# Eleven short warming products, two more ahead of the fifth block, and block loads that wait for an earlier load

## The chip, the cores and the metric

The kernel runs on one core of one Trainium2 chip. The metric is device time in microseconds (us). The engines are TensorE (PE, with its weight loads as PEld), VectorE (DVE), ScalarE (ACT), GpSimd (POOL) and SyncE (SP), whose queue (SPq) issues nearly all DMAs here.

## The reference

Three stages in a row, on 1536 tokens (2 batches of 768) with 8 heads of 64:

```python
state = gamma * state + k_t outer v_t          # per head, token after token
y_t   = scale * q_t . state                    # retention
x = y as (1536, 512)
h = x @ w_in;  g = h * tanh(softplus(h));  x = g @ w_out          # 512 -> 2048 -> 512
x = (sigmoid(x @ w_gate) * (x @ w_val)) @ w_out2                  # 512 -> 1536 -> 512
```

All weights come as 64-bit floats.

## The kernel before, in words

**Retention** works on 12 blocks of 128 tokens, six for each batch. A block needs two loads of 512 KB: `qk` (queries and keys, features on partitions) and `nv` (keys and values, tokens on partitions). They land in the pool `ld`, which has four buffers of each (`AHEAD = 4`). POOL scales the values by the decay table `ck` (`at_prep`, tile `vp`). PE makes the scores (`sc`), DVE masks them into `a`, PE adds the block's keys times `vp` to the running state (`st`, in PSUM), ACT copies the state out (`s`, in `keep`), and PE makes the output (`ao`) from `a` with `vp` and from `qk` with `s`. DVE multiplies `ao` by the decay `og` into `acc`.

Blocks 0 to 3 (the first four, `T = 4`) are written one after another with products over 128 tokens (`at_scores`, `at_state`, `at_out`). From block 4 (the fifth) a block's scores and state are made in two halves of 64 tokens, of 64x64 products (`scores`, `state`, `outs`), and the products of two blocks alternate (`lanes`, `block`). Between such blocks stand pieces of the first MLP (`dense`, tiles `hx` and `h`, `SHARE[n]` pieces after a block).

**Weights** arrive as pieces of 128 x 512 64-bit words (`raw`, 512 KB, two buffers, `load_piece`). ACT and DVE turn a piece into a 32-bit tile `v`, and ACT and DVE or POOL split that into a high and a low part (`ww`, `wo`).

**Order.** Each engine's instructions keep the order in which the code issues them (`Queue.issue` chains each to the one before). All of the retention stage is in that written order: loads first (`load(0)` to `load(3)`), then after block j of the first four `load(j + 4)`, and in the later loop `load_nv(j + 4)`, `load_qk(j + 3)` and the next weight piece (`feed`). SP issues them in this order, and a DMA waits in SP's queue for its buffer to be free. After the blocks, the rest (both MLPs) is collected as nodes and put in order by a planner (`replay`) from fixed costs.

**Warming products.** Before block 0, PE multiplies a tile of zeros (`z`) by itself five times, 128 x 128 by 128 x 256, into two PSUM buffers that nothing reads. A product of plain 32-bit operands shows as two weight loads and two passes in the trace, so these five are ten rows of each.

The helper `issue` is the one place that calls an engine, so nearly every row of the trace is at its line, L147; groups are told apart by their tiles.

Of the kernel before, what the change touches and what calls it, by code (L numbers as in the profile page):

```python
# [9 lines left out]
F32 = mybir.dt.float32  # L10
# [8 lines left out]
P = 128  # L19
# [4 lines left out]
def kernel(ctx, tc, qk, nv, w1i, w1o, w2g, w2v, w2o, ma_in, og_in, sg_in, ck_in, mh_in, out):  # L24
# [14 lines left out]
    NP = KK  # L39
    D = P // 2  # L40
    FF1 = w1i.shape[0]
    FF2 = w2g.shape[0]
    N = 512
# [3 lines left out]
    RINGS = {"w": 7, "o": 4, "q": 2}  # L47
    H = DM // 2
    STG = 2
    WARM = 5  # L50
    AHEAD = 4
    Q = P // 2
    SHARE = (4, 4, 3, 3, 2, 2, 4, 5, 5)
# [117 lines left out]
    pe = Queue(nc.tensor, lambda n, kw: (kw["rhs"].at.size + 32) / 2400, 0.2)  # L171
    dve = Queue(nc.vector, span(0.1, 0.00102), 0.2)
    act = Queue(nc.scalar, lambda n, kw: 0.14 + 0.0008 * min(n, N), 0.2)
    pool = Queue(nc.gpsimd, slow, 0.2)
    sync = Queue(nc.sync, lambda n, kw: 1.4 if isinstance(kw["out"], Part) else 1.6, 3.5)
# [120 lines left out]
    ps_o = Pool(name="ps_o", bufs=2, space=PSUM)  # L296
# [46 lines left out]
    for f in range(FF2):  # L343
# [3 lines left out]
        a, q, w, o = [[(k, (2, f))] for k in "aqs"] + [[("o", (2, f - 1)), ("o", (2, f))] if f % 2 else []]  # L347
# [103 lines left out]
    def flush_hi():  # L451
        while late_hi:
            late_hi.pop(0)()
# [7 lines left out]
    def pump(n=1):  # L461
        if not early:
            flush()
        for _ in range(n):
            if not steps and not plan():
                return
            ring = steps[0][0]
            if not room(ring) if ring else "dcs" not in lo_eng:
                return
            steps.pop(0)[1]()  # L470
# [59 lines left out]
    hx = {}  # L530
# [215 lines left out]
    def run(*parts):  # L746
        for p in parts:
            for s in p:
                s()
# [22 lines left out]
    with ExitStack() as actx:  # L772
        ac = actx.enter_context(tc.tile_pool(name="ac", bufs=1))
# [8 lines left out]
        ck = ac.tile([P, SPB, 2 * NP, 1], F32, name="ck")  # L782
        sg = ac.tile([P, SPB, NP, 1], F32, name="sg")
        og_t = [ac.tile([P, NP, P], F32, name=f"og{b}") for b in range(SPB)]
        qk_t, nv_t, a_t, vp_t, st_t, s_t, sc_t, o_t = {}, {}, {}, {}, {}, {}, {}, {}

        def load_qk(j):
            if j < NSUB:
                qk_t[j] = ld.tile([P, 2, NP, P], F32, tag="qk", name="qk_t")
                sync.dma_start(out=qk_t[j], in_=qk[j])  # L790

        def load_nv(j):
            if j < NSUB:
                nv_t[j] = ld.tile([P, 2, 2 * NP, D], F32, tag="nv", name="nv_t")
                sync.dma_start(out=nv_t[j], in_=nv[j])

        def load(j):
            load_qk(j)
            load_nv(j)
# [14 lines left out]
        def rows(n):  # L814
            return slice(Q * n, Q * n + Q)

        def quarter(o, w, x, start=True, stop=True):
            pe.matmul(out=o, lhsT=w, rhs=x, start=start, stop=stop, skip_group_check=True)
# [24 lines left out]
        def state(j, s):  # L843

            if j >= NSUB:
                return [lambda: [quarter(st_t[0][rows(c), 0, :], z[rows(0), rows(0)], z[rows(0), rows(0)]) for c in range(2)]]
            v, k = vp_t[j], nv_t[j]
            new = j % SPB == 0 and s == 0
            if new:
                st_t[0] = ps_s.tile([P, NP, D], F32, tag="s", name="st")  # L850
            st = st_t[0]

            def pair(p):
                for e in range(2):
                    quarter(st[rows((e + p) % 2), p, :], k[rows(s), 0, 2 * p + e, :], v[rows(s), 2 * p + e, :],
                            new and p == 0, p == NP - 1)

            return [lambda p=p: pair(p) for p in range(NP)]

        def keep(j, s):  # L860
            s_t[2 * j + s + 1] = at6.tile([P, NP, D], F32, tag="s", name="s")
            act.activation(out=s_t[2 * j + s + 1], in_=st_t[0], func=AF.Copy)
# [95 lines left out]
        act.activation(out=sig, in_=one_t, func=AF.Mish)  # L958
        z = ac.tile([P, NP * D], F32, name="z")
        dve.memset(ap=z, constant=0.0)  # L960
        for n in range(WARM):
            o = ps_o.tile([P, NP * D], F32, tag="o", name="warm")
            pe.matmul(out=o, lhsT=z[:, 0:P], rhs=z)
        def work(n):
            for _ in range(n):
                dense.pop(0)()
# [11 lines left out]
        for j in range(T):  # L978
# [13 lines left out]
            if j == T - 2:  # L992
                pump()
        flush_hi()
        run(state(T, 0))
        keep(T, 0)
        lanes(scores(T + 1, 0), scores(T + 1, 1))
# [9 lines left out]
        decays(T)  # L1007
        decays(T + 1)
        load_nv(T + AHEAD)
        pump()  # L1010
        work(SHARE[0] - 1)
# [5 lines left out]
        for j in range(T + 1, NSUB + 1):  # L1017
            block(j, middles.get(j, lambda: None))
            load_nv(j + AHEAD)
            load_qk(j + AHEAD - 1)  # L1020
            if j < NSUB and j != 2 * SPC:
                feed()
            if j == NSUB:
                flush()
            for n in range(SHARE[j - T]):
                if j == NSUB:
                    lo_eng["g"] = dve if n > 2 else pool
                    run(late_g)
                    late_g.clear()
                work(1)  # L1030
# [24 lines left out]
    for i in range(I0, L1 + 1):  # L1055
        n = len(rest) if i < L1 else 8
# [17 lines left out]
    for f in range(2, FF2):  # L1074
        n = 4 if f < 4 else 6
# [3 lines left out]
        if f == FF2 - 1:  # L1079
            n = 3  # L1080
# [64 lines left out]
```

## Time and profile before

| | us |
|---|---|
| three runs | 581.82, 583.6, 579.15 |
| their median | 581.82 |
| the profiled execution, its own time | 578.88 |
| its span, first to last instruction | 577.0 |
| PE busy in it | 568.1 (98%) |

The profiled execution has 1.9 us beside its span. In the rows, "x" is a count, times are us from the span's start, "idle before <-releaser" is how long the engine waited ahead of the row and what ended that wait, and PEclk or the clock column is the granted clock of TensorE as a share of its upper level.

### The profile page before, as it was taken

To read this page: it belongs to the slowest core of one execution; us is meant where nothing else is said; L and a number is where in the kernel's file an instruction comes from. 1 tells how busy PE (TensorE), PEld (TensorE's weight loads), DVE (VectorE), ACT (ScalarE), POOL (GpSimd) and SP (SyncE) were. 2 spreads that over 40 slices of the span, in tenths; PEclk is the share of its full clock that TensorE was granted. 3 is DMA by queue.
4 is the path that set the end of the run, shared out by engine and by line. 5 is a ranking of instruction groups with operands and counts; after the bars stand their busy time and mean duration, and the time that the engine had idled before them with its cause. 6 is when DMAs were issued, how large, how long until landed. Compare 5 with 4: busy or idle time off the path is not lost.

```text
span 577.0 us, 9810 instructions
## 1 busy us (share of the span) xinstructions
PE 568.1 (98%) x3880; PEld 479.2 (83%) x3880; DVE 458.9 (80%) x680; ACT 294.4 (51%) x544; POOL 219.1 (38%) x198
## 2 busy tenths in 40 slices
PE   8899999999999999999999999999999999999997
PEld 6777888888888888888888878888888888888885
DVE  3877599898998787778988888789888788775574
ACT  1566677585645545355665677545346254231210
POOL 3455588533522300024597554423245043020000
PEclk9999999999999999999999999999999999999999
DMA  9984202422332222112100233221322222000014
GB/s 344 404 294 159 76 0 74 136 86 77 105 110 73 74 73 74 37 39 108 37 1 0 91 128 111 74 87 59 110 74 73 74 73 74 1 0 2 0 38 181
DMA packets 15741, 52.40 MB, mean 91 GB/s; under 512 B 2128, under 2 KB 2256, under 8 KB 15696
## 3 DMA queue, kind: packets, MB, share of 16 engines
q1 hardware_dynamic: 14976, 51.39, 25.5%
q8 instruction: 30, 0.49, 0.3%
q10 hardware_dynamic: 720, 0.40, 0.2%
q14 instruction: 15, 0.12, 0.1%
HBM read 48.63 MB, written 3.15 MB: 90 GB/s over the span
## 4 chain that ended last, share of the span: by engine, by line
PE 95%; DMA 3%; DVE 1%; issue 0%; POOL 0%; SPq 0%; ACT 0%; POOLq 0%; DVEq 0%
PE h L147 37%; PE o L147 37%; PE hx L147 17%; DMA nv_t<-nv 3%; PE ao L147 2%; PE st L147 1%; PE sc L147 1%; DVE h L147 0%; POOL vp L147 0%; SPq L147 0%; DVE acc L147 0%; DVE ww L147 0%; ACT e L147 0%; POOLq L147 0%; DVEq L147 0%
## 5 line engine op out<-in xcount | busy, mean ns | idle before, releaser
L147 PE MATMUL o<-g,wo 128*128 128x512 f32 x492 | 119.1, 391 | 0.0
L147 DVE TENSOR_TENSOR acc<-o,acc 128x512 f32<-128x512 f32 x126 | 86.9, 690 | 39.5 <-PE o L147 37.7
L147 PE MATMUL o<-wo,g 128*128 128x512 f32 x432 | 108.6, 392 | 0.0
L147 PEld LDWEIGHTS o<-g,wo 128*128 128x128 f32 x492 | 90.3, 188 | 17.4
L147 PE MATMUL h<-B,ww 128*128 128x512 f32 x372 | 94.4, 390 | 0.0
L147 PE MATMUL h<-T,ww 128*128 128x512 f32 x366 | 92.9, 390 | 0.1
L147 PEld LDWEIGHTS o<-wo,g 128*128 128x128 f32 x432 | 78.5, 189 | 14.7 <-DVE g L147 0.3
L147 PEld LDWEIGHTS h<-T,ww 128*128 128x128 f32 x366 | 68.4, 188 | 15.1 <-ACT e L147 0.5
L147 PEld LDWEIGHTS h<-B,ww 128*128 128x128 f32 x372 | 68.9, 188 | 13.9
L147 DVE SCALAR_TENSOR_TENSOR raw<-raw 128x512 int32<-128x512 int32 x68 | 61.9, 912 | 2.2 <-ACT raw L147 2.0
L147 ACT ACTIVATE raw<-raw 128x512 int32<-128x512 uint8 x68 | 45.6, 670 | 34.3 <-DMA raw<-w2v 9.1
L147 DVE SCALAR_TENSOR_TENSOR v<-v,raw 128x512 int32<-128x512 int32 x68 | 58.5, 865 | 3.1 <-ACT v L147 0.8
L147 PE MATMUL hx<-xc,ww 128*128 128x256 f32 (+1 forms) x342 | 58.3, 307 | 0.0
L147 POOL TENSOR_TENSOR ww<-s,ww 128x512 fp32r<-128x512 f32 x22 | 30.1, 1371 | 67.8 <-ACT ww L147 67.8
L147 PEld LDWEIGHTS hx<-xc,ww 128*128 128x128 f32 x342 | 50.6, 190 | 5.4 <-DVE ww L147 0.3
L147 POOL TENSOR_TENSOR wo<-v,wo 128x512 fp32r<-128x512 f32 x16 | 21.1, 1330 | 86.2 <-ACT wo L147 49.7
L147 DVE TENSOR_TENSOR h<-h,u 128x512 f32<-128x512 f32 x54 | 37.6, 697 | 15.9 <-PE h L147 14.9
L147 ACT ACTIVATE e<-h 128x512 f32<-128x512 f32 x29 | 17.3, 596 | 59.4 <-PE h L147 48.2
L147 ACT ACTIVATE v<-raw 128x512 f32<-128x512 f32 x68 | 45.1, 666 | 2.1 <-POOL wo L147 1.2
L147 PEld LDWEIGHTS hx<-YT,ww 128*128 128x128 f32 x270 | 38.3, 190 | 3.5
L147 PE MATMUL hx<-YT,ww 128*128 128x256 f32 x270 | 39.4, 282 | 0.0
L147 ACT ACTIVATE g<-h 128x512 fp32r<-128x512 f32 x53 | 31.4, 597 | 14.9 <-DVE h L147 13.9
(97 smaller groups left out, 836.4 us busy)
## 6 DMA issues: line engine op xcount, KB each, us to landing
raw<-w1i SPq DMA_DIRECT2D x16, 512.0 KB, 3.3
raw<-w1o SPq DMA_DIRECT2D x16, 512.0 KB, 3.4
qk_t<-qk SPq DMA_DIRECT2D x12, 512.0 KB, 6.7
nv_t<-nv SPq DMA_DIRECT2D x12, 512.0 KB, 6.8
raw<-w2g SPq DMA_DIRECT2D x12, 512.0 KB, 3.2
raw<-w2v SPq DMA_DIRECT2D x12, 512.0 KB, 3.3
raw<-w2o SPq DMA_DIRECT2D x12, 512.0 KB, 3.3
out<-acc SPq DMA_DIRECT2D x12, 256.0 KB, 2.0
```

The source lines that it names most:

```text
L147: i = call(**kw)
```

## The change

There are three parts:

- The five warming products of 256 columns become eleven of 128 columns, all into one PSUM buffer.
- Two more such products stand on PE between the scores of block 4 and its first state product `state(T, 0)`. They write the PSUM bank `x0`.
- Every load of `qk` or `nv` is noted in `sent`. From the fifteenth on (`qk` of block 7 is the first), SP first issues a copy of one 32-bit word into the new tile `mark`, read from the tile that was noted two entries earlier. The copy can't be issued before the load that fills this tile has landed, and the block's load stands behind the copy in SP's queue. With the current load counted, that is the third one back.

```diff
-    WARM = 5
+    WARM = 11
...
+        mark, sent = ac.tile([P, 32], F32, name="mark"), []
...
+        def paced(t):
+            sent.append(t)
+            if len(sent) > 2 * AHEAD + 6:
+                n = len(sent) % 32
+                sync.dma_start(out=mark[:1, n:n + 1], in_=sent[-3][:1])
...
                 qk_t[j] = ld.tile([P, 2, NP, P], F32, tag="qk", name="qk_t")
+                paced(qk_t[j][:, 0, 0, :1])
                 sync.dma_start(out=qk_t[j], in_=qk[j])
...
                 nv_t[j] = ld.tile([P, 2, 2 * NP, D], F32, tag="nv", name="nv_t")
+                paced(nv_t[j][:, 0, 0, :1])
                 sync.dma_start(out=nv_t[j], in_=nv[j])
...
-        for n in range(WARM):
-            o = ps_o.tile([P, NP * D], F32, tag="o", name="warm")
-            pe.matmul(out=o, lhsT=z[:, 0:P], rhs=z)
+        def warm(pool, tag, n):
+            o = pool.tile([P, N], F32, tag=tag, name="warm")
+            for _ in range(n):
+                pe.matmul(out=o[:, :P], lhsT=z[:, :P], rhs=z[:, :P])
+
+        warm(ps_o, "o", WARM)
...
         flush_hi()
+        warm(hx["pool"], "x0", 2)
         run(state(T, 0))
```

On PE the difference stands in two places. At the program's start (`warm` is the warming product, `sc` and `st` are scores and state of block 0):

```order
-L147 MATMUL warm<-z 128x256 x5
+L1154 UNCONDITIONAL_BRANCH
+L147 MATMUL warm<-z 128x128 x11
 L147 MATMUL sc<-qk_t 128x128 x8
 L147 MATMUL st<-vp,nv_t 64x64 x8
```

Five products became eleven of half the width, and what follows is as before. At the fifth block (`ao` ends block 3, `sc` are the scores of block 4, then its first state product and the scores of block 5):

```order
@@ -17,4 +17,5 @@
 L147 MATMUL ao<-qk_t,s 64x128 x8
 L147 MATMUL sc<-qk_t 64x64 x16
+L147 MATMUL warm<-z 128x128 x2
 L147 MATMUL st<-vp,nv_t 64x64 x8
 L147 MATMUL sc<-qk_t 64x64 x16
```

Two products came in between scores and state, and nothing changed places. On SP, from the loads of block 6 on (`qk_t` and `nv_t` are block loads, `raw` is a weight piece, `mark` the small copy):

```order
 L147 DMA qk_t<-qk 128x1024
 L147 DMA nv_t<-nv 128x1024
+L147 DMA mark<-qk_t 1x1
 L147 DMA qk_t<-qk 128x1024
+L147 DMA mark<-nv_t 1x1
 L147 DMA nv_t<-nv 128x1024
 L147 DMA raw<-w1i 128x512
+L147 DMA mark<-qk_t 1x1
 L147 DMA nv_t<-nv 128x1024
 L147 DMA raw<-w1i 128x512
+L147 DMA mark<-nv_t 1x1
 L147 DMA nv_t<-nv 128x1024
```

Ten copies came in, each ahead of a block load; the last stands ahead of `qk` of block 11. On DVE, ACT and POOL, and on PE elsewhere, the rows are those of before in the same order.

## Rows read from the trace of the kernel before

**Rows 1.** The page: busy time per engine, TensorE's clock and DMA in 40 slices.

```profile
PE 568.1 (98%) x3880; PEld 479.2 (83%) x3880; DVE 458.9 (80%) x680; ACT 294.4 (51%) x544; POOL 219.1 (38%) x198
...
PEclk9999999999999999999999999999999999999999
DMA  9984202422332222112100233221322222000014
```

**Rows 2.** Busy us by stretch: PE, PEld, DVE, ACT, POOL, then clock, DMA share, GB/s.

```profile
2.00:16.00 14.00, 13.14 (x184) 10.77 (x184) 5.93 (x12) 2.63 (x5) 6.62 (x7) 1.00 1.02 395
...
30.00:50.00 20.00, 18.84 (x568) 15.00 (x564) 14.65 (x25) 13.77 (x29) 9.47 (x8) 1.00 0.84 294
...
60.00:577.00 517.00, 513.10 (x2579) 434.74 (x2578) 417.98 (x613) 263.45 (x481) 191.46 (x171) 1.00 0.20 68
```

**Rows 3.** The chain that ended last, 9 to 24 us: start, us, what.

```profile
10.00 9.48 DMA nv_t<-nv
...
19.64 1.05 POOL vp L147
...
22.59 0.49 issue
```

**Rows 4.** The warming products alone: ns min/median/max, first and last start.

```profile
L147 PEld LDWEIGHTS warm<-z x10: 204/337/337, 1.2 to 4.8; 128*128 128x128 f32 x10
L147 PE MATMUL warm<-z x10: 379/634/793, 1.2 to 5.0; 128*128 128x256 f32 x10
```

**Rows 5.** PE in order of time, 0 to 30 us: start, us, what.

```profile
1.22 4.18 PE L147 MATMUL warm<-z 128*128 128x256 f32 x10 [1.22 <-DVE z L147]
5.33 1.16 PE L147 MATMUL sc<-qk_t 64*128 64x128 f32 x16
6.95 0.69 PE L147 MATMUL st<-vp,nv_t 128*64 128x64 f32 x16 [0.46 <-POOL vp L147]
7.67 1.16 PE L147 MATMUL sc<-qk_t 64*128 64x128 f32 x16
...
10.22 0.69 PE L147 MATMUL st<-vp,nv_t 128*64 128x64 f32 x16 [0.36 <-POOL vp L147]
...
20.73 0.62 PE L147 MATMUL st<-vp,nv_t 64*64 64x64 f32 x14 [0.93 <-POOL vp L147]
```

**Rows 6.** SP's queue in order of time: loads of blocks 6, 6, 7, weights, block 8.

```profile
17.04 0.33 SPq L147 DMA_DIRECT2D qk_t<-qk  x1
17.45 0.38 SPq L147 DMA_DIRECT2D nv_t<-nv  x1
19.42 0.33 SPq L147 DMA_DIRECT2D qk_t<-qk  x1
...
20.32 0.38 SPq L147 DMA_DIRECT2D raw<-w1i  x1
22.67 0.33 SPq L147 DMA_DIRECT2D nv_t<-nv  x1
```

**Rows 7.** us from issue to landing, issues at 17.04, 17.45, 20.32, 22.67, 29.10.

```profile
qk_t<-qk SPq DMA_DIRECT2D x1, 512.0 KB, 7.6
...
nv_t<-nv SPq DMA_DIRECT2D x1, 512.0 KB, 8.4
...
raw<-w1i SPq DMA_DIRECT2D x1, 512.0 KB, 9.4
...
nv_t<-nv SPq DMA_DIRECT2D x1, 512.0 KB, 8.3
...
raw<-w1i SPq DMA_DIRECT2D x1, 512.0 KB, 3.3
```

**Rows 8.** POOL, then ACT in order of time: who takes these loads.

```profile
29.94 1.04 POOL L147 TENSOR_TENSOR vp<-nv_t,ck 128x512 f32<-128x512 f32 x1
...
34.97 1.04 POOL L147 TENSOR_TENSOR vp<-nv_t,ck 128x512 f32<-128x512 f32 x1 [2.29 <-PE ao L147]
...
31.18 0.66 ACT L147 ACTIVATE raw<-raw 128x512 int32<-128x512 uint8 x1
...
34.18 0.60 ACT L147 ACTIVATE e<-h 128x512 f32<-128x512 f32 x1 [1.78 <-PE h L147]
```

**Rows 9.** The chain at 48 us, and the stretches between two "issue" waits.

```profile
48.00 0.73 issue
...
23.08:29.38 6.30, 6.30 (x127) 4.96 (x127) 5.89 (x7) 4.63 (x10) 3.49 (x4) 1.00 0.96 380
...
48.73:52.58 3.85, 3.84 (x127) 3.09 (x126) 2.42 (x4) 2.75 (x6) 3.39 (x3) 1.00 0.05 16
```

## The prediction

> **What bounds the kernel now.** I read the page first. PE is busy 98% of the span, at its upper clock level in all 40 slices, and the DMA engines are full or nearly so only in the first three slices [rows 1]. So a change of start-up products and of load times can only be worth something where PE stands still, and the stretches say where that is: from 60 us on PE is idle 3.9 us out of 517, which leaves 568.1 - 513.1 = 55.0 us of work in the first 60 us, and 5.0 us of idle time there [rows 1, 2]. All three parts of the change lie in these 60 us. Filling every gap in them would give 5.0 us, 0.9% of the time. I take 1% (5.8 us) as what a measurement of this kernel can tell from no change, its three runs lying 4.5 us apart; so a visible gain would need more than all that is there.
>
> Next, what holds PE in these 60 us. From 2 to 16 us the DMA engines have a share of 1.02 at 395 GB/s [rows 2]: the first loads are bound by the transfer rate, not by when they are asked for. The chain that ended last shows it: the load of `nv` of block 4 is asked for at 10.00 and takes 9.48 us, POOL makes `vp` of it at 19.64, and only then, after 0.93 us of waiting, PE begins the state product of block 4 at 20.73 [rows 3, 5]. Whatever PE does faster or slower before 19.80 is cut off or swallowed there. Later the idle time of PE is mostly what the profile calls "issue", 0.49 us at 22.59 and 0.73 us at 48.00 [rows 3, 9], which is neither a load nor another engine.
>
> **The eleven short products.** Before, ten passes over 256 columns take 4.18 us [rows 5]. The weight loads among them have a median of 337 ns and a least of 204 ns [rows 4]: nearly all ran at the lower of the two clock levels, 1.2 GHz, and the last at 2.4 GHz, though the clock column says 1.00 throughout. After, there are 22 passes over 128 columns, that is 2816 columns for 2560. If the columns set the pace, a pass takes half of 0.418 us, 0.21 us, and 22 of them 4.6 us: the scores of block 0 start at about 5.8 us in place of 5.33, or earlier by what the last passes save at the upper level; I take 0.3 us late. If the weight load sets the pace (337 ns, then 204 ns) some ten passes are done by 4.8 us, where the last of the old weight loads began, and twelve remain, 2.4 us: the scores start near 7.2 us, 1.9 us late. The first end is the nearer, since in the rows the passes are 0.42 us apart and the weight load of 337 ns lies wholly under the pass before it. Of the delay nothing reaches the end at first: PE waits 0.46 us at 6.95, 0.36 us at 10.22 and 0.93 us at 20.73 for POOL [rows 5], 1.75 us together. So this part costs 0, and at its upper bound 0.1 to 0.2 us.
>
> **The two more.** They are four passes at the upper level, at half the lower level's 0.21 us, so 0.42 us, or 0.82 us by the weight load's 204 ns. They stand in the queue exactly ahead of the product that waits 0.93 us for `vp` [rows 5], so they fill that wait: cost 0. If the eleven had used the wait up already (both upper ends), 1.9 + 0.82 - 1.75 = 1.0 us would show. What they can win is the clock, if it falls in this wait in some executions; in the profiled one it does not fall, and there the gain is 0.
>
> **The paced loads.** Ten copies, each an issue of about 0.33 to 0.38 us on SP [rows 6], 3.5 us of an engine that is far from full. What counts is what they hold back: behind a copy stand the block's load, and behind that weight pieces and all later loads. No row shows such a copy, so I follow the queue with the times of the rows.
>
> Before, `qk` and `nv` of block 6 are asked for at 17.04 and 17.45 and land 7.6 and 8.4 us later, at 24.64 and 25.85 [rows 6, 7]. The first copy reads that `qk`, so `qk` of block 7 is asked for at 24.64 + 0.35 = 25.0, not at 19.42. That is 5.6 us later, but its long time to landing was queueing: with little ahead of it a load takes 3.3 us [rows 7], so it lands at about 28.3, where before it came between 25.85 and the weight piece. `nv` of block 7 waits for 25.85, is asked for at 26.3, and lands one load's time later at 29.6 (25.85 - 24.64 = 1.2, so I take 1.3 us). The weight piece behind it, asked for at 20.32 and landed at 29.7 before [rows 6, 7], now goes out at 26.7 and lands at 30.9. `nv` of block 8, before 22.67 + 8.3 = 31.0, waits for 28.3, goes out at 28.7 and lands at 32.2.
>
> So these landings slip by about 1.2 us, and now the question is who is waiting. POOL takes `nv` of block 7 at 29.94, straight after other work, and that of block 8 at 34.97, when PE frees a buffer; ACT takes the weight piece at 31.18 and later stands idle 1.78 us at 34.18 [rows 8]. All are later than 29.6, 32.2 and 30.9. From there on the buffers, not the copies, mostly say when a load may go, and fewer transfers stand ahead of it. I put this part at 0. Its upper bound is the rival below; the bound below zero comes from the code fetch, next.
>
> **The extra code on PE.** The "issue" waits have a pattern: between the waits ending at 23.08 and 29.38 lie 127 products and 127 weight loads, between those ending at 48.73 and about 52.58 there are 127 and 126 [rows 9]. With a semaphore instruction or two that is 256, so PE stops where a block of its code of that size ends. There are four such waits, 1.5 us in all. The change adds 6 x 2 x 2 = 24 PE instructions at the start and 8 at block 4 (each product is two loads and two passes, and six products more plus two). The ends of the code blocks thus come 32 instructions earlier in the work, which at 256 per 3.85 to 6.3 us [rows 9] is 0.5 to 0.8 us. The fetch is begun that much earlier as well, so I expect the waits to stand elsewhere with much the same sum: 0, between -1.5 us (all gone) and +2.1 us (five of 0.73 in place of 1.5).
>
> The Trainium skill, "Runtime: NRT & Kernel Launch", section "Instruction fetch mechanics", says that code is refilled in blocks of 256 instructions and that the cost of crossing a block is mostly hidden. The rows agree on the size and not on the hiding: a crossing cost 0.73 us at 48.00 [rows 9]. By its rule the shift would be worth nothing, which is also the value that I take.
>
> **The sum.** 0 + 0 + 0 + 0 on the execution of 578.88 us. That execution is not the typical run: the others took 579.15, 581.82 and 583.6 us. Its rows hold nothing that lasts 3 to 5 us longer in some executions, so I cannot tell which part of the program spreads. The middle of the four is (579.15 + 581.82) / 2 = 580.5, 1.3 us under the median of the three. With no change in the kernel's own path I forecast that middle, **580.4 us**.
>
> **Rivals.** First, the spread is the clock. If in some executions PE's clock rises later at the start, or falls in the wait at 20 us, the longer warming and the two more products remove it, and the median comes down to what the profiled execution took, 578.9 us, perhaps 578.4 with a code wait less. For it: the first 3.5 us did run at the lower level [rows 4, 5], and the gaps are where the products were put. Against it: the profiled execution shows no fall, and 10% more columns are little. The Trainium skill, "TensorE: Matmul & The Clock Gate", section "Part 1: The HAM clock gate (the "warmup" mystery)", says that the number of slow products at the start differs from run to run of one kernel, and that the ramp penalty is under 1% of a typical span; the first half speaks for this rival, the second bounds it, and no run here shows either yet.
>
> Second, slower: the pacing starves POOL. It needs that a load takes 7 to 8 us even with only two under way, as the rows of the full queue have it [rows 7]. Then `qk` of block 7 lands at 25.0 + 7.6 = 32.6, `nv` of block 8 goes out at 33.0 and lands at 41.3, 6.3 us after POOL wants it at 34.97 [rows 8], and each later block adds some more, since two loads in 8 us feed one block, and blocks 4 to 11 at most fill the stretch from 20.73 to 60 us, 4.9 us each. Some 6 to 10 us would show: 588 us. It decides from the point where two such loads in a row exceed 34.97 - 25.0 = 10 us, 5 us each. Against it stands the 3.3 us of a load with an empty queue, and 0.84 as the DMA share from 30 to 50 us [rows 2], which leaves room.
>
> Third, the change doesn't do what it says: the copies hold nothing, since buffers already do. That gives the forecast's time, 580.4, and differs only in the trace.
>
> **How the numbers follow.** I give the forecast and the third rival 0.70, the clock 0.22, starving 0.05, and 0.03 to something unseen on either side. The range must cover the clock rival and the spread of the runs: from 577.4 (578.9 less 1.5 of code waits) to 583.6, the slowest run seen and also the forecast plus the upper ends of code, pace and start (2.1 + 1.0). A median under 576.0 would need more than PE's idle time gives: 0.03. Over 587.6 needs the starving: 0.05. Within 1%: 0.92.
>
> **What would show it.** In the changed profile: warming ends between 5.4 and 5.9 us; the two products lie inside the wait before 20.7, and that state product starts within 0.2 us of where it did; `qk` of block 7 is asked for near 25 us and lands near 28 us, a time to landing of 3 to 4 us in place of 7 to 8; POOL's `vp` at 34.97 still waits for PE; "issue" waits of 1 to 2 us in all stand 32 instructions earlier. I am wrong if a `vp` row names a DMA as its releaser after 30 us, if the eleven products push the start of block 4's state past 21.5, or if runs of both kernels on the same chip differ by more than the spread shown.

## The result, and the profile after

| | before | after |
|---|---|---|
| median of 15 runs each, us | 580.68 | 584.06 |
| lowest and highest, us | 578.99, 583.6 | 581.54, 587.96 |
| the profiled execution, its own time | 578.88 | 585.96 |
| its span | 577.0 | 584.2 |

The ratio is 1.0054 with a 95% interval of [1.0039, 1.0068]: the changed kernel is 2.3 to 3.9 us slower. That is less than 1%, and 0.5 us beyond the upper end of the range. The profiled execution of after lies 1.9 us above its median and that of before 1.8 us below, so the two spans differ by 7.2 us where the medians differ by 3.4.

The page of after, busy time of PE, then clock and DMA in 40 slices, answers to [rows 1]:

```profile
PE 571.6 (98%) x3896; PEld 482.8 (83%) x3896; DVE 458.1 (78%) x680; ACT 294.6 (50%) x544; POOL 219.7 (38%) x198
...
PEclk9899999999999999999999999999999999999999
DMA  9785302232233030303100233322313222000004
```

Stretches of after, columns as in [rows 2]:

```profile
2.00:16.00 14.00, 12.87 (x188) 11.33 (x188) 5.57 (x11) 2.63 (x5) 6.27 (x7) 1.00 1.02 396
...
24.90:28.40 3.50, 3.50 (x12) 2.60 (x9) 3.50 (x5) 2.77 (x6) 1.86 (x2) 0.51 0.40 145
...
30.00:50.00 20.00, 16.98 (x528) 13.44 (x526) 11.81 (x21) 10.91 (x23) 8.14 (x7) 1.00 0.81 294
37.51:43.78 6.27, 4.69 (x128) 3.58 (x129) 3.69 (x6) 2.93 (x6) 2.58 (x2) 1.00 0.79 270
55.60:59.20 3.60, 3.60 (x79) 3.17 (x70) 2.01 (x4) 3.13 (x7) 3.60 (x4) 0.53 0.02 5
60.00:584.00 524.00, 520.39 (x2792) 441.01 (x2784) 423.62 (x621) 268.44 (x491) 192.75 (x172) 1.00 0.21 68
```

From 60 us on PE is idle 3.6 us, as before (3.9), so all of the loss lies in the first 60 us. There PE works 571.6 - 520.4 = 51.2 us and is idle 8.8, where it was idle 5.0. From 30 to 50 us it works 16.98 us in place of 18.84. Two stretches of 3.5 us run at half the clock, that is at 1.2 GHz, which the trace of before does not have.

The chain that ended last says what the idle time is:

```profile
24.97 3.94 PE hx L147 x9
...
36.10 1.41 issue
...
42.20 1.58 issue
...
52.52 2.25 issue
...
57.49 2.35 PE hx L147 x6
...
64.83 0.20 PE st L147 x2
```

and in the chain of before the same nine passes:

```profile
24.63 2.29 PE hx L147 x9
```

The waits called "issue" come to 6.0 us (these three, and 0.78 us at 22.34), where they were 1.5: 4.5 us more. The nine passes of `hx` at 24.97 took 3.94 us in place of 2.29, and the six at 57.49 took 2.35, where six others of the same trace took 1.58 at 61.87: 1.65 and 0.77 us for the low clock. Together 6.9 us. The two state products at 64.83 stood at 57.58 before, 7.25 us earlier, so this is nearly the whole difference of the two executions. It is an account of these two executions, though, and not yet of the medians. The stretch from 37.51 to 43.78 lies between two "issue" waits and holds 128 products and 129 weight loads, so these waits still stand at the ends of code blocks, as in [rows 9]; they are called code waits below.

PE in order of time in after, which answers to [rows 5], and its warming weight loads, to [rows 4]:

```profile
1.22 4.27 PE L147 MATMUL warm<-z 128*128 128x128 f32 x22 [1.22 <-DVE z L147]
5.42 1.16 PE L147 MATMUL sc<-qk_t 64*128 64x128 f32 x16
...
20.09 0.71 PE L147 MATMUL warm<-z 128*128 128x128 f32 x4
20.84 0.62 PE L147 MATMUL st<-vp,nv_t 64*64 64x64 f32 x14
...
L147 PEld LDWEIGHTS warm<-z x26: 186/333/333, 1.2 to 20.4; 128*128 128x128 f32 x26
```

The scores of block 0 begin 0.09 us later than before, and the state of block 4 0.11 us later. SP's queue in order of time, which answers to [rows 6]:

```profile
25.15 0.71 SPq L147 DMA_DIRECT2D mark<-qk_t  x1
25.96 0.34 SPq L147 DMA_DIRECT2D qk_t<-qk  x1
26.40 0.60 SPq L147 DMA_DIRECT2D mark<-nv_t  x1
27.10 0.33 SPq L147 DMA_DIRECT2D nv_t<-nv  x1
27.53 0.39 SPq L147 DMA_DIRECT2D raw<-w1i  x1
...
35.10 0.58 SPq L147 DMA_DIRECT2D mark<-nv_t  x1
35.73 0.38 SPq L147 DMA_DIRECT2D qk_t<-qk  x1
```

The copies do hold the loads: `qk` of block 7 goes out at 25.96 (19.42 before). But they hold the later ones too. `qk` of blocks 8 to 11 is asked for at 35.73, 41.97, 47.13 and 50.45; in the trace of before at 30.00, 35.30, 40.06 and 44.54. After, from block 9 on, then before, from block 8 on:

```profile
41.97 0.33 SPq L147 DMA_DIRECT2D qk_t<-qk  x1
47.13 0.34 SPq L147 DMA_DIRECT2D qk_t<-qk  x1
50.45 0.37 SPq L147 DMA_DIRECT2D qk_t<-qk  x1
...
30.00 0.38 SPq L147 DMA_DIRECT2D qk_t<-qk  x1
35.30 0.33 SPq L147 DMA_DIRECT2D qk_t<-qk  x1
40.06 0.42 SPq L147 DMA_DIRECT2D qk_t<-qk  x1
44.54 0.33 SPq L147 DMA_DIRECT2D qk_t<-qk  x1
```

The times from issue to landing of `qk` of block 7 and `nv` of blocks 7 and 9 (issues at 25.96, 27.10, 33.20), which answer to [rows 7]:

```profile
qk_t<-qk SPq DMA_DIRECT2D x1, 512.0 KB, 3.1
...
nv_t<-nv SPq DMA_DIRECT2D x1, 512.0 KB, 5.4
...
nv_t<-nv SPq DMA_DIRECT2D x1, 512.0 KB, 5.5
```

`nv` of block 8 took 5.2 us and `qk` of block 8 5.5. POOL and ACT, who take these loads, against [rows 8]:

```profile
32.66 1.19 POOL L147 TENSOR_TENSOR vp<-nv_t,ck 128x512 f32<-128x512 f32 x1 [1.64 <-DMA nv_t<-nv]
...
33.82 0.67 ACT L147 ACTIVATE raw<-raw 128x512 int32<-128x512 uint8 x1 [0.92 <-DMA raw<-w1i]
```

Both now wait for a load, and take it 2.7 and 2.6 us later than before. From 20 us on PE waits for no load in this execution.

### The profile page after: what moved, and what is told of

It is laid out like the page before. It is cut to its first block, busy times and chain, and to the rows that moved or that the text cites. A ratio compares the mean times of both kernels' runs of the same rounds, so it can differ in the third digit from the quotient of the medians.

```text
span 584.2 us, 9863 instructions
## 1 busy us (share of the span) xinstructions
PE 571.6 (98%) x3896; PEld 482.8 (83%) x3896; DVE 458.1 (78%) x680; ACT 294.6 (50%) x544; POOL 219.7 (38%) x198
## 4 chain that ended last, share of the span: by engine, by line
PE 96%; DMA 1%; issue 1%; DVE 0%; SPq 0%; POOL 0%; ACT 0%; DVEq 0%
PE h L147 37%; PE o L147 36%; PE hx L147 17%; PE ao L147 2%; PE st L147 2%; DMA nv_t<-nv 1%; PE sc L147 1%; DVE h L147 0%; SPq L147 0%; POOL vp L147 0%; DVE acc L147 0%; PE warm L147 0%; ACT e L147 0%; DVEq L147 0%
## 5 line engine op out<-in xcount | busy, mean ns | idle before, releaser
L147 PE MATMUL hx<-xc,ww 128*128 128x256 f32 (+1 forms) x342 | 60.0, 312 | 0.0
L147 DVE TENSOR_TENSOR h<-h,u 128x512 f32<-128x512 f32 x54 | 37.6, 697 | 16.0 <-PE h L147 15.1
L147 ACT ACTIVATE g<-h 128x512 fp32r<-128x512 f32 x53 | 31.4, 597 | 14.9 <-DVE h L147 13.9
```

What stands on the lines that cost most here:

```text
L147: i = call(**kw)
```

## The experiments

Two questions had to be told apart: which of the three parts costs, and by what way (loads that come too late, the copies on SP, the shifted code, the clock). Times are medians; "before" is the kernel before in the same session. Over all these sessions 69 of 89 runs of the kernel before had a mean granted clock of 0.999 or 1.000 (full clock, below) and a median of 579.9 us, and the 20 with a lower one had 582.3; where a kernel's runs divide unevenly, the text tells them apart.

**The loads alone (pace_only).** The kernel before with only the copies:

```diff
+                sync.dma_start(out=mark[:1, n:n + 1], in_=sent[-3][:1])
```

> The copies and their waits alone, with the five old warming products and none at block 4. Measured so far: before 580.7 us, changed kernel 584.1 us, 3.4 us apart; in the changed kernel's trace PE's code waits ('issue') are 6.0 us in the first 60 us in place of 1.5, and the clock fell twice. Theory A (the waits behind the copies shift transfers, and PE pays): about 584, code waits well over 1.5 us. Theory B (the copies as extra DMAs slow PE's code fetch): about 584 too. Theory C (the 32 added PE instructions move the ends of code blocks to worse places): 580.7, no change.

Measured: 582.68 against 579.88, ratio 1.0046 [1.0024, 1.0067]; the runs at full clock 582.14 against 579.77. So this part carries 2.8 of the 3.4 us by the medians, and 2.4 us at full clock, so most of it is not the clock. Theory A put the loss into code waits; this trace has only 0.6 us of them from 20 to 66 us. Here the chain from 24 to 66 us names the load itself, of blocks 8, 9 and 10, and PE's waits from 20 to 66 us name it too:

```profile
36.15 4.38 DMA qk_t<-qk
...
41.23 5.99 DMA qk_t<-qk
...
47.96 5.62 DMA qk_t<-qk
...
PE sc L147 <- DMA qk_t<-qk: 5.1, 3, 2.2
```

PE's scores waited three times for `qk`, 5.1 us in sum, the longest 2.2.

**The warming products alone (warm_only).** Eleven and two, no copies:

```diff
-    WARM = 5
+    WARM = 11
...
+        warm(hx["pool"], "x0", 2)
```

> The eleven short products and the two more, no copies. Theories A and B: no change, 580.7 us, or up to 1.5 us less if the clock was what spread the runs. Theory C: about 584, with code waits of 5 us or more.

Measured: 581.22 against 579.88, ratio 1.0011 [0.9997, 1.0026]. No difference that can be told, at most 1.5 us; its trace has code waits of some 3.6 us in place of 1.5, with no load held back and none added, so a small loss by the shifted blocks is possible.

**The eleven alone (eleven_only).** As warm_only without the line of the two.

> Only the eleven short products in place of the five (24 PE instructions more at the start), no two more, no copies. Theories A and B: 580.7 us. Theory C: slower by some part of 3.4 us, since 24 of the 32 added instructions are here.

Measured: 580.33 against 579.88, ratio 1.0005 [0.9981, 1.003]. The longer warming makes no difference that can be told.

**Copies that wait for nothing (copies_no_wait).** As pace_only, but the copy reads a tile that has long been there:

```diff
-                sync.dma_start(out=mark[:1, n:n + 1], in_=sent[-3][:1])
+                sync.dma_start(out=mark[:1, n:n + 1], in_=ck[:1, 0, 0, :])
```

> As pace_only, but each copy reads the decay table, which has long landed, so the ten copies are issued and nothing waits for an earlier load. Theory B: as pace_only, about 584. Theory A: as before, 580.7, within 0.5 us. Theory C: 580.7.

Measured: 580.05 against 579.88, ratio 1.0012 [0.9993, 1.0032]. Ten copies of some 0.6 us each on SP cost nothing that can be told (579.48 against 579.77 us at full clock); what costs in pace_only is that they hold the loads back.

**How deep (pace_second, pace_fourth, pace_fifth).** pace_only with the copy reading one nearer, or one or two further back, so that one, three or four block loads may be under way:

```diff
-                sync.dma_start(out=mark[:1, n:n + 1], in_=sent[-3][:1])
+                sync.dma_start(out=mark[:1, n:n + 1], in_=sent[-2][:1])
```

> Old warming products; a block's load waits for the load right before it (one under way in place of two). Rate theory: with two under way a pair of loads took 5.2 to 5.7 us to land plus 0.7 us for the copy, 6.2 us a block, where PE does a block in 4.7; with one under way a block needs two loads one after the other, some 4.2 + 0.7 us each, 9.8 us. The ten loads from 25 us on would end near 75 us and the kernel take about 600 us (592 to 605). Rival (a held load costs once, because the first is asked for 5.6 us later): about 583, as with two under way.

> Old warming products; three loads under way. Rate theory: three loads in 6.2 us are two in 4.1 us, less than a block of PE (4.7 us), so the loads keep up and the time is that of before, 579.9 us, within 0.7 us. Rival (held once): slower by 1.5 us or more, since the first loads are still asked for 3 us later than before.

> Old warming products; four loads under way. Rate theory: as before, 579.9 us, within 0.5 us. Rival (held once): between before and pace_fourth.

Measured, against 580.15: 595.09 with one, ratio 1.0255 [1.0232, 1.0278]; 581.07 with three, 1.0009 [0.9988, 1.003]; 579.91 with four, 0.9997 [0.998, 1.0013]. With two it was 1.0046. At full clock three took 579.74 and four 579.65, before 579.95; by the medians three lie 0.9 us above before, where at most 0.7 was expected. The loss falls from 14.9 us over 2.8 to nothing that can be told; of the 14.9 some 2 us may be the clock's, all four of those runs being below full clock. The chain of pace_second from 30 us shows the cause most plainly, one load after another with a copy between, and PE's waits (20 to 70 us) name `qk` for 10.6 us:

```profile
26.94 3.07 DMA qk_t<-qk
...
30.03 0.60 SPq L147
...
30.72 3.21 DMA nv_t<-nv
...
42.53 4.13 DMA qk_t<-qk
...
PE sc L147 <- DMA qk_t<-qk: 10.6, 4, 4.5
```

A load by itself takes 3.1 to 3.3 us, and 4.1 to 4.2 with a weight piece beside it. In pace_fourth the waits of PE in the same stretch name no load, and `qk` of block 8 goes out at 30.77, close to the 30.00 of before.

**Only some of the copies (pace_first_four, first_four_again, last_six).** For the first four the condition is

```diff
-            if len(sent) > 2 * AHEAD + 6:
+            if 2 * AHEAD + 6 < len(sent) <= 2 * AHEAD + 10:
```

and for the last six it is `len(sent) > 2 * AHEAD + 10`.

> As pace_only (two under way), but only the first four of the ten copies: ahead of the two loads of block 7, nv of block 8 and nv of block 9. Rate theory: the delay builds up load after load, and the later loads, unpaced, catch up, since DMA has room: about 580.5 us (579.8 to 581.3). Rival (held once): as pace_only, 582.7 us, since the hold at 25 us is all there.

> The first four copies alone once more, on another chip or at another hour, to have enough runs at full granted clock (two of eight had it the first time). Theory (two loads under way carry less than PE takes, block after block, so a short paced stretch costs little): the runs at full clock lie within 0.8 us of before's at full clock, about 580.5, and the median's excess over that is the clock. Rival (the first paced blocks carry the whole loss): about 582.5 at full clock too.

> Only the last six copies, from the queries and keys of block 8 on. Theory (the loss accumulates with the paced blocks): these six blocks' loads start from a full queue and lose part of the 2.8 us of all ten, 580.5 to 581.8 us. Rival (the first paced blocks carry the whole loss): within 0.4 us of before. If it costs the whole 2.8 us, it is the last six alone that matter, at the place where PE waited for qk of blocks 8 to 10.

Measured: the first four 582.92 against 580.15, ratio 1.004 [1.0021, 1.0058], which is the rival's figure. But only two of these eight runs had the full clock, and they took 580.25 and 580.95. In the second session, 582.07 against 581.4, ratio 1.0016 [0.9999, 1.0033], and 581.61 against 580.80 at full clock (5 and 20 runs). At full clock, then, the first four cost 0.7 to 0.8 us in both sessions; by the medians the sessions give 2.8 and 0.7 us. The last six: 581.76 against 581.4, 1.0017 [0.9998, 1.0035], and 580.81 against 580.80 at full clock. That is the rival's figure here, not the theory's. At equal clock neither stretch alone makes up the 2.8 us. That the loss comes only where the whole row of blocks is paced fits this, but it is not shown: the intervals are as wide as the effect, and few of the runs had the full clock.

**The change with three under way (after_fourth).**

```diff
-                sync.dma_start(out=mark[:1, n:n + 1], in_=sent[-3][:1])
+                sync.dma_start(out=mark[:1, n:n + 1], in_=sent[-4][:1])
```

> The changed kernel with the copy reading the load one further back, so that three may be under way. Theory (the loss is the depth alone): within 0.8 us of the kernel with the warming products alone, 580.3 to 581.5 us, with PE waiting for no load of qk. Rival (the parts add up to more together than apart, through the code blocks that the added products shift): 582.5 us or more although no load is waited for.

Measured: 581.78 against 581.4, ratio 1.0015 [0.9999, 1.0031]. PE names no load of `qk` in its waits. One number brings the changed kernel back to within the measurement of before, so the depth is the cause of most of the loss; the interval leaves up to 1.8 us for anything else. That the parts make each other worse is not seen either: pace_only and warm_only come to 2.8 + 1.3 us by their medians, the whole change to 3.4.

**More transfers, no pacing (extra_loads).** The trace of after had no wait of PE for a held load, but long "issue" waits at the ends of code blocks. To see whether queued transfers can make these, the kernel before got six loads that nobody reads (the tile is overwritten later):

```diff
+            for n in range(0, 4 if 5 <= j <= 7 else 0, 2):
+                sync.dma_start(out=acc_t[2][:, n:n + 2], in_=qk[n].rearrange("p a b c -> p a (b c)"))
```

> The kernel before with six more loads of 512 KB in SP's queue, two each after the loads that follow blocks 5, 6 and 7. They go into an accumulator tile that is written later and that nothing has read by then, so nothing waits for them, and the output is the same. Theory (code is fetched through the same DMA engines and stands behind what is queued there): the 'issue' waits of PE between 30 and 60 us, about 1.0 us in sum before, rise to 3 to 6 us, and the median to 582 to 585 us. Rival (only the landing time of a block's own load counts, and the loads have slack): issue waits within 0.7 us of before's, time within 1 us of before, about 580. If PE names a DMA of qk or POOL one of nv as its releaser instead, the extra megabytes cost through the loads, and the test tells nothing of the code.

Measured: 584.76 against 581.4, ratio 1.0059 [1.0037, 1.0081], or 3.4 us. In the trace PE waits for no DMA, and its chain has

```profile
39.48 1.44 issue
...
45.42 1.79 issue
...
51.39 2.10 issue
```

where before had none, 0.09 and 0.73 us at the same three ends of code blocks. At equal clock the runs are 2.4 us (below full) and 3.1 us (full, two runs) longer than those of before. The code that PE fetches shows as packets of a queue of its own ("instruction", q8): each trace has 30 of 16 KB for some 7800 products and weight loads. After the wait that ended at 47.22 the queues carried, from 47.3 to 50.7 and from 50.7 to 51.2:

```profile
DMA packets 384, 1.40 MB, mean 412 GB/s; under 512 B 42, under 2 KB 42, under 8 KB 384
...
q8 instruction: 1, 0.02, 13.4%
```

In the first stretch there is no such packet, in the second there is one: it came some 3.7 us after PE had passed the end of a code block. In before, at the same place, PE passed the end at 43.82 and the packet came between 46.2 and 46.5, 2.5 us later. PE had the same code to run in both, for 4.2 us; the queues carried 413 GB/s over it in extra_loads and 318 in before. In after, from the end passed at 37.51, it came between 41.4 and 41.8:

```profile
DMA packets 314, 1.15 MB, mean 303 GB/s; under 512 B 33, under 2 KB 33, under 8 KB 314
...
q8 instruction: 1, 0.02, 14.9%
```

the first line being of 37.6 to 41.4, which has no such packet. In all three PE goes on 2.2 to 2.6 us after the packet begins. So here more transfers under way delay the code, and PE loses time even where it waits for no load. For the kernel before this is shown by extra_loads, which added only transfers; that the code waits of after have the same cause rests on the packet's time alone. Against it stand warm_only, with waits of 1.12 and 1.43 us at two such ends, and last_six, with one of 1.51 us at 22.97, before its first copy goes out at 32.11: long code waits come without pacing too.

## Why the prediction was wrong

**Warming products and the two more: right.** They were put at no cost; the start moved 0.09 us where 0.3 was taken, the two lie in the wait, and warm_only and eleven_only show no difference. The 22 passes took 4.27 us, near the 4.6 us of the columns, and ended at 5.49, inside the 5.4 to 5.9 that were to show it.

**The paced loads: the step that failed.** It read: "From there on the buffers, not the copies, mostly say when a load may go, and fewer transfers stand ahead of it. I put this part at 0." I followed the queue through four loads, as far as `nv` of block 8, found every consumer later than the landing (by 0.3 us for two of them), and stopped. Those landings were already too early: `nv` of blocks 7 and 8 landed at 32.5 and 35.1 where 29.6 and 32.2 were worked out, and the `vp` row at 32.66 that names a DMA after 30 us is one of the prediction's own signs of being wrong. The copies went on to hold each later load, and `qk` of block 8 went out 5.7 us later than before. The sizes used were wrong too. A copy was taken at 0.35 us and took 0.58 to 0.71. And "with little ahead of it a load takes 3.3 us", the next 1.3 us more: that row was of one load beside a nearly empty queue. With two block loads and a weight piece or two under way most loads took 5.2 to 5.7 us. Before's own block loads in that stretch (issues from 29.52 to 44.54) took 5.5 to 7.0, so the single load got no slower; but before asks for the next without waiting, and the paced queue doesn't. Two loads in that time, and a copy after each, is a block in 5.1 to 6.7 us (`qk` of pace_only goes out at 36.15, 41.23 and 47.96), where before's are asked for every 4.5 to 5.3 us. The difference adds up from block to block, as the second rival said, but PE met it at `qk`, not at `nv`.

**The starving rival: near the mechanism, wrong in place and price.** It decides "from the point where two such loads in a row exceed 34.97 - 25.0 = 10 us, 5 us each". The two that it means, `qk` of block 7 and then `nv` of block 8, took 3.1 and 5.2 us, 9.1 from the first issue to the last landing at 35.08, and POOL took that `nv` only at 38.04, when PE had freed a buffer. So its condition was not met there, and the loads of `qk` that PE waited for in pace_only went out later. It was priced at 588 us from loads of 7.6 us, those of the full queue; by the spacing of `qk` in pace_only, (47.96 - 36.15) / 2 = 5.9 us a block against (40.06 - 30.00) / 2 = 5.0 in before, it would have been 0.9 us a block, some 3.5 us over blocks 8 to 11, near the 2.8 found. It got 0.05 of the chance because the single load, and the DMA share of 0.84 from 30 to 50 us, were taken to speak against it; in pace_only that share was 0.83, with PE waiting for loads all the same.

**The code waits: right in place, missed in cause.** The shift of 32 instructions by itself stayed within its bounds of -1.5 to +2.1 us (warm_only). That the waits could grow because loads delay the fetch was not considered. In the profiled after they are 4.5 us more; warm_only has 2.1 of that without pacing, and what made the rest is not separated. The Trainium skill, "Runtime: NRT & Kernel Launch", section "Instruction fetch mechanics", calls the cost of crossing a block mostly hidden. The trace of extra_loads says otherwise: 1.4 to 2.1 us at three crossings.

**The sum's base and the clock.** The median of before over 15 runs was 580.68 where 580.4 was taken. The clock rival was right that runs below full clock are longer (579.9 and 582.3 us, above) and wrong on the cure: with both sets of warming products, 4 of 12 runs of warm_only were below full clock, 9 of 15 of after. Nor is the clock the main of the loss: the six runs of after at full clock have a median of 583.6 us.

**The third rival** (the copies hold nothing) fell with copies_no_wait against pace_only.

**What stays open.** In the execution of pace_only the 2.8 us show as waits for `qk`, in that of after as code waits and a lower clock, with the same pacing. One can cover the other: in after, `qk` of block 8 landed at 41.27, and PE, held up by two code waits and the low clock, came to that block's scores at 43.95; in pace_only it stood ready at 39.81 and waited to 40.67. How a typical run divides between the two is not shown. Nor is it settled why after has more runs below full clock. Over all the kernels whose copies hold loads these were 57 of 99 runs, against 13 of 36 with the other parts alone and 20 of 89 of before, so a comparison at full clock may leave out a part of what the pacing costs. Of the clock's two falls in the trace of after the second comes 0.9 us after the 2.25 us wait, and that of extra_loads at 52.9 us, in its 2.10 us wait; the first, at 25 us, also stands at 24 us in copies_no_wait and eleven_only, and there no load is held back.

## What to carry to other kernels

A load's long time to landing in a full queue was not slack here that could be given away: count what the consumers take per block, and follow the held queue to its last load, not to the first few that seem to arrive in time. Try a limit on loads under way at several depths: here one cost 14.9 us, two 2.8, and three and four nothing that could be told. And where an engine runs long straight code, look for "issue" waits at regular counts of instructions: in extra_loads added transfers made them longer.

## What was not expected of the hardware

- Data transfers delayed the code of PE: the packet came 2.5 us after the end of a block before, 3.7 us after it with 3 MB more loaded in the neighbourhood, and PE stood up to 2.1 us for it (extra_loads).
- A 512 KB load took 3.1 us alone, 4.1 to 4.2 beside one weight piece and 5.2 to 5.7 in company of another block load and pieces, and 7.6 to 8.6 in the queue of before at 17 to 23 us, 5.5 to 7.0 from 29.5 us on. So with two under way a load did not keep the time of a single one. From 20 to 30 us, where the first loads are held, the queues moved 245 GB/s in after and 368 in before; from 30 to 50 us, 294 in both.
- In 20 of 89 runs of the unchanged kernel the mean granted clock is below full, and such a run is some 2.3 us longer by the medians. In the traces here that have such a fall, it is to half, for 3.4 to 6.8 us at a time.
